# A fused attention and feed-forward kernel: its planner's order replaced by a table of placements

## The chip, the cores and the metric

The kernel runs on 1 core of one Trainium2 chip. The metric is the device time of one execution in microseconds (us), taken as the median of 3 runs. The kernel before has a median of 208.76 us (208.06 to 209.29).

The core has these engines, each with its own queue of instructions that runs in order: TensorE for matmuls (PE in the profile, PEld for its weight loads), VectorE (DVE), ScalarE (ACT), GpSimd (POOL) and SyncE (SP, which only issues DMAs here). PSUM, where matmuls write, has 8 banks. An instruction starts when it is at the head of its engine's queue and the semaphores that it waits for have been raised.

## The reference

```python
B, H, S, D = 4, 8, 768, 64            # n_sink = 4, window = 128
scores = scale * q @ k.T               # per batch and head
keep = (pos_k < 4) | (0 <= pos_q - pos_k < 128)
a = softmax(where(keep, scores, -1e9)) # over keys
x = merge_heads(a @ v)                 # (4, 768, 512)
xn = (x - mean) / sqrt(var + 1e-6) * g_ln
out = x + relu(xn @ w_ch1) @ w_ch2     # 512x2048, then 2048x512; float32 out
```

Each query sees the 128 latest keys and the first four keys of its batch (the sinks). What follows is a layer norm without a bias, two layers of weights with a ReLU between them, and the sum with x.

## The kernel before

**Tiles and chunks.** The 3072 tokens are 24 tiles of 128 tokens (t = 0 to 23), six for each batch, and 12 chunks of two tiles (c = 0 to 11; chunk c has tiles 2c and 2c+1). All matmuls are in bf16 with sums in fp32. The three big inputs are loaded tile by tile in bf16 (by GpSimd's queue, which casts on the way; L589 for v, L626 and L687 for q and k), apart from the first tile, whose q and k come in fp32 on SyncE (L620) and are cast on chip (cast0, cast1, L637).

**Attention.** For each tile or chunk: q and k are transposed (on TensorE for chunks 0 to 3, L645 and L672, with copies out of PSUM named ev..., L595; by DMA on SyncE from chunk 4, helper L569); scores (sc, L754 for one tile, L802) go into a pair of PSUM banks; ScalarE makes the exponents (ex, L758 and L814); VectorE or GpSimd multiplies by a mask (mk, L761, L826, L821); the values are weighted by matmuls (av, L854); the sinks have scores, exponents and values of their own (sx and sv, L714 and L721). ev10 and ev11 are the copies of the transposed q and k of chunk 1, ev010 and ev011 those of the second tile. For the sinks, kts is a small buffer of the sinks' keys (kts0 is the copy at L695), pick is a constant that spreads them, and vc holds the sinks' values of the later batches: vc0 clears it (VectorE, L511) and vcd stands for 16 small loads into it on SyncE (L535).

**Layer norm.** VectorE divides by the sum (rc, L868, and x, L870) and takes mean and variance (bn, L874, and ag); GpSimd takes the power -0.5 (rs, L882; it reads the constant mhalf); xc (L885) is x less the mean. Then x is transposed: for chunks 0 and 1 on TensorE (trx, L893) with a copy that multiplies by g (evx, L907, by the four columns gt, L531); from chunk 2 by a DMA on SyncE (trx, L569). The result is xnt.

**The two layers.** Layer 1 makes ph0 to ph7 (L1020 by tile for chunks 0 and 1, so that ph0_0 needs tile 0 alone and ph0_1 tile 1; L1027 later; the name is ph, then the chunk, then the number). From chunk 4, half of them is replaced by seven smaller products m1 to m7 with fewer multiplications (L958), whose sums run on VectorE, ScalarE and GpSimd. A ReLU (rl, L1037 on ScalarE, L1039 on VectorE) moves each ph to hq. From chunk 2 layer 2 is seven products p1 to p7 (L1109, 8 matmuls each) in the place of eight: sums s1 to s4 of blocks of hq (VectorE, L1092) and differences of w2 are multiplied; tm (L1123) adds x, o (L1130) makes the last sum of a quarter of 128 tokens by 256 columns, each on VectorE. For p6 the sum s2 of both halves is needed, and s2 needs s1 and the ReLUs of ph4 to ph7. o11_0 to o11_3 are the four quarters of chunk 11.

**Stores.** All go out on SyncE: whole tiles of 128x512 in fp32 (256 KB; L1070, L1159) and quarters of 128x256 (128 KB; L1154) for the first tile of some chunks and both tiles of the last. st20 and st21 are the stores of tiles 20 and 21 (chunk 10), st220, st221, st232 and st233 the four quarters of tiles 22 and 23. At the very end, gsum and late are single tiny matmuls, and guard is a check of the softmax sums; if it failed, a slow general version in a branch would run. It doesn't for these inputs.

**What sets the order.** The body doesn't issue instructions as it goes. It describes 1137 operations with `P.op(name, engines with durations, priority, emit, reads, writes, ...)`, and `Plan.run` then places them: a list scheduler with a cost of each operation on each engine that may run it, a priority (mostly the time at which it is due), rings of buffers, latencies between engines, and a model of the DMA queues. It gives each operation an engine and a start, and a buffer slot for each buffer. At the end all operations are sorted by that start and emitted, and each engine runs its own in that order. So a planned start is no command to wait: it sets only who stands ahead of whom on an engine. Gaps of TensorE in the first 24 us of the plan are filled with junk matmuls (L1236) that no operation needs.

Of the kernel before, what the change touches and what calls it, by code (L numbers as in the profile page):

```python
# [64 lines left out]
class Plan:  # L65


    SEM = 0.035
    TO_PE = 0.11
    PE_DRAIN = 0.18  # L70
    SWITCH = 0.095
    LANES = 8
    SHARED = 36.0
    MIXED = 1e9
    DMA_BUSY = {}

# [31 lines left out]
    def lat(self, src, dst):  # L108
        if src.eng == "PE" and src.dma is None:
            return -self.PE_DRAIN if dst == "PE" else self.SEM  # L110
        return self.TO_PE if dst == "PE" else self.SEM

    WINDOW = {"PE": 0.2, "ACT": 0.25, "DVE": 0.25, "POOL": 0.25, "SP": 0.0}

    def run(self):
        free = {"PE": 0.9, "ACT": 0.75, "DVE": 0.9, "POOL": 1.5, "SP": 0.75}
        lanes = {"POOL": [0.0] * self.LANES, "HW": [0.0] * self.LANES}
        n_dma = {"POOL": 0, "HW": 0}
        dma_free = {"POOL": 0.0, "HW": 0.0, "all": 0.0}
        mode = "n"  # L120
        ready = [o for o in self.ops if o.n_wait == 0]
        order = []
        tensor = sorted((o for o in self.ops if "PE" in o.engs), key=lambda o: (o.prio, o.seq))
        while ready:
            while tensor and tensor[0].start is not None:
                tensor.pop(0)
            head = tensor[0] if tensor else None
            cand = {}
            first = min([o.prio for o in ready for b in o.bufs if b.ring == "pair" and b.slot is None], default=1e9)
            for o in ready:  # L130
                if "PE" in o.engs and o is not head and o.prio >= PAR["strict"]:
                    continue
                need = [b for b in o.bufs if b.ring and b.slot is None]
                ok, avail, took = True, 0.0, {}
                for b in need:
                    used = [u for s in took.values() for u in s.units]
                    ss = [s for s in self.rings[b.ring] if not s.held and not any(u in used for u in s.units)
                          and not (s.lent and o.prio > first)]
                    if not ss:
                        ok = False  # L140
                        break
                    since = max([min(s.free_at for s in ss)] + [min(free[e] for e in o.engs) - 0.3])
                    s = min((s for s in ss if s.free_at <= since), key=lambda s: (s.rank, s.free_at))
                    took[b] = s
                    avail = max(avail, s.free_at)
                if not ok:
                    continue
                best = None
                for e, (occ, lat) in o.engs.items():
                    r = max([free[e], o.nb, avail + (self.TO_PE if e == "PE" else self.SEM)]  # L150
                            + [d.end + self.lat(d, e) for d in o.deps])
                    if e == "PE" and o.mode_in != mode:
                        r = max(r, free[e] + self.SWITCH)
                    if o.dma is not None:
                        q = "POOL" if e == "POOL" else "HW"
                        r = max(r, lanes[q][n_dma[q] % self.LANES])
                    if best is None or r + lat < best[0] - 1e-9:
                        best = (r + lat, e, r)
                cand.setdefault(best[1], []).append((best[2], o, took))
            if not cand:  # L160
                stuck = sorted(ready, key=lambda o: o.prio)[:8]
                raise RuntimeError("plan stuck: " + ", ".join(
                    f"{o.name}[{','.join(b.name for b in o.bufs if b.ring and b.slot is None)}]" for o in stuck))
            e = min(cand, key=lambda e: min(c[0] for c in cand[e]))
            t0 = min(c[0] for c in cand[e])
            st, o, took = min((c for c in cand[e] if c[0] <= t0 + self.WINDOW[e]), key=lambda c: (c[1].prio, c[1].seq))
            for b, s in took.items():
                b.slot = s
                s.take()
            o.eng, o.start = e, st  # L170
            occ, lat = o.engs[e]
            free[e] = st + occ
            if e == "PE":
                mode = o.mode_out
            if o.dma is None:
                o.end = st + lat
            else:
                busy, first, last = o.dma
                q = "POOL" if e == "POOL" else "HW"
                if st < self.MIXED:  # L180
                    at = max(st + occ + first, dma_free[q], dma_free["all"] if st < self.SHARED else 0.0) + busy
                    dma_free[q] = dma_free["all"] = at
                    o.end = at + last
                else:
                    real = self.DMA_BUSY.get(o.dma, busy)
                    other = dma_free["HW" if q == "POOL" else "POOL"] > st + occ + first
                    at = max(st + occ + first, dma_free["all"]) + real
                    dma_free[q] = dma_free["all"] = at
                    o.end = at + last + max(0.0, busy - real) + (PAR["mix"][q == "POOL"] if other else 0.0)
                lanes[q][n_dma[q] % self.LANES] = o.end  # L190
                n_dma[q] += 1
            for b in o.bufs:
                b.left -= 1
                if b.left == 0 and b.ring:
                    b.slot.give(min(u.start for u in b.users), max(u.end for u in b.users))
            ready.remove(o)
            order.append(o)
            for s in o.succ:
                s.n_wait -= 1
                if s.n_wait == 0:  # L200
                    ready.append(s)
        assert len(order) == len(self.ops), "cycle in the plan"
        order.sort(key=lambda o: (o.start, o.seq))
        return order


def pe(us):
    return {"PE": (us, us + Plan.PE_DRAIN)}

# [15 lines left out]
SW = (0.9, 0.7, 0.9)  # L225
# [7 lines left out]

Plan.DMA_BUSY = {SW: 1.03, HW_X: 0.55}

LOW, HIGH = 1e-9, 1e9
NEG = -1e30
NEVER = -1e9

# [134 lines left out]
def kernel(  # L374
# [157 lines left out]
    for g in range(4):  # L532
        for hh in range(4):
            p0 = 32 * g + NS * hh
            P.op(f"vcd{g}{hh}", {"SP": (0.3, 0.3)}, 3.2 + 0.01 * (4 * g + hh), lambda e, p0=p0, h=4 * (g % 2) + hh: nc.sync.dma_start(  # L535
                vc[p0:p0 + NS, 1:B, 0:64], v[1:B, h, 0:NS, :].rearrange("b s d -> s b d")),
                reads=[Bc["vc"]], writes=[Bc["vcd"]], dma=HW_T, nb=30.0)
# [67 lines left out]
    def chunk(c):  # L605
# [74 lines left out]
        else:  # L680
            for x, (nm, src) in enumerate((("k", k), ("q", q))):
                for i in range(2):
                    nat = Buf(f"{nm}n{c}{i}", "nat")
                    ap = src[b, :, 256 * R + 128 * i:256 * R + 128 * (i + 1), :].rearrange("h p d -> p h d")
                    soon = c >= PAR["half"] + 3 and x == 0 and i < PAR["soon"]
                    loads[2 * c + i, nm] = P.op(f"{nm}ld{c}{i}", {"POOL": (0.87, 0.9)}, ld + 0.01 * i + 0.1 * x,
                         lambda e, nat=nat, ap=ap: G.dma_start(nat.t, ap), writes=[nat], dma=SW if c < 6 else (*SW[:2], PAR["llag"]), after=behind(c, 0 if soon else 1))  # L687
                    loads[2 * c + i, nm].soon = soon
                    P.op(f"tr{nm}{c}{i}", {"SP": (1.2, 1.2)}, d + 0.01 * i, lambda e, nat=nat, i=i, x=x: dma_t(
                        T.t[:, :, x, 128 * i:128 * i + 128], nat.t.rearrange("p h d -> p (h d)")),  # L690
                        reads=[nat], writes=[T], dma=HW_X, after=[scores[c - 1]])
# [152 lines left out]
    def value(c, i, pes, ps, d, part, srcs, po=None):  # L844
# [49 lines left out]
        if c >= PAR["x_by_dma"]:  # L894
            P.op(f"trx{t}", {"SP": (1.2, 1.2)}, d + 0.5, lambda e: dma_t(xnt_b[c].t[:, :, 128 * i:128 * i + 128], xc.t),
# [110 lines left out]
    def mlp(c):  # L1006
# [38 lines left out]
        for i in range(2):  # L1045
# [5 lines left out]
            for f in range(parts):  # L1051
# [17 lines left out]
                P.op(f"st{t}{f}", {"ACT" if parts == 2 and not f else "SP": (0.35, 0.4)}, T + 4 * i + 3.6,  # L1069
# [4 lines left out]
    def wino(c, T, hq, h1, quick):  # L1074
# [76 lines left out]
        for half in (0, 2, 3, 1) if c == NC - 1 else (0, 1) if c in PAR["split"] else ():  # L1151
            t, sl = 2 * c + half // 2, slice(256 * (half % 2), 256 * (half % 2) + 256)
            b, r = t // RB, t % RB
            P.op(f"st{t}{half}", {"SP": (0.35, 0.4)}, 3000.0 + half % 2 if c == NC - 1 else u(6), lambda e, i=half // 2, b=b, r=r, sl=sl: nc.sync.dma_start(  # L1154
                out[b, 128 * r:128 * (r + 1), sl], ots[i].t[:, sl]), reads=[oo[half]], hold=[ots[half // 2]], dma=HW_S)
        for i in () if c == NC - 1 else (1,) if c in PAR["split"] else (1, 0):
            t = 2 * c + i
            b, r = t // RB, t % RB
            P.op(f"st{t}", {"SP": (0.35, 0.4)}, u(5 if i else 6), lambda e, i=i, b=b, r=r: nc.sync.dma_start(  # L1159
# [120 lines left out]
```

## Time and profile before

| | |
|---|---|
| median of 3 runs | 208.76 us (208.06 to 209.29) |
| span of the profiled execution | 206.6 us |
| so around the span | 2.16 us |
| TensorE busy | 199.4 us, 97% of the span |
| VectorE busy | 179.6 us, 87% |
| ScalarE busy | 119.7 us, 58% |
| GpSimd busy | 118.7 us, 57% |
| DMA over the span | 27.55 MB, 133 GB/s in the mean |

The profile is of one execution. Its own time isn't given apart from its span; the median of the runs, taken without a profile, stands 2.16 us above that span. A line of code in the profile is that of the kernel before, given as L and its number. A row of a timeline is start, duration, engine, line, operation, and output<-inputs by the buffers' names; a bracket at its end is the time for which the engine had stood idle and what ended that. A row of the groups has the busy time and the mean in ns behind the bar, and then the idle time before the group. The buffer names join many operations: `one` and `pair` are the PSUM rings, `kq` the transposed q and k, `xnt` the transposed tokens, `hq` the hidden layer, `hs` the sums s1 to s4, `ot` the output.

### The profile page before, as it was taken

How to read it: one execution, taken by the hardware profiler on the slowest of the kernel's cores; microseconds unless marked ns; L12 is line 12 of the kernel's file. 1: busy time of each engine (PE TensorE's matmuls, PEld its weight loads, DVE VectorE, ACT ScalarE, POOL GpSimd, SP SyncE). 2: the span in 40 equal slices, each digit the busy share in tenths (PEclk: the TensorE clock that was granted, in tenths of full speed). 3: DMA queues.
4: the chain of work that ended last, by engine and by line, in shares of the span. 5: the costliest groups of instructions: out<-in, count | busy, mean ns of one | idle time of the engine just before them, and what ended most of it. 6: DMA issues, size and time to landing. Idle time of an engine off the chain costs nothing.

```text
span 206.6 us, 6790 instructions
## 1 busy us (share of the span) xinstructions
PE 199.4 (97%) x2766; PEld 165.6 (80%) x2766; DVE 179.6 (87%) x437; ACT 119.7 (58%) x187; POOL 118.7 (57%) x170
## 2 busy tenths in 40 slices
PE   6888999999999999999999999999999999999994
PEld 2557996674698897898998988988988988988993
DVE  7589769899599899899989989989989989998693
ACT  3649477839555655666486486485486585560620
POOL 7977475279039029959649949968627229125000
PEclk9999999999999999999999999999999999999999
DMA  5999999999999999999999999899976411210302
GB/s 117 146 195 195 197 181 205 199 158 171 186 200 124 124 191 101 121 174 101 175 152 137 113 159 143 109 171 114 194 117 101 128 33 23 106 32 19 108 27 84
DMA packets 101341, 27.55 MB, mean 133 GB/s; under 512 B 89652, under 2 KB 99128, under 8 KB 101304
## 3 DMA queue, kind: packets, MB, share of 16 engines
q0 software_dynamic: 67712, 13.37, 81.7%
q1 hardware_dynamic: 33304, 13.43, 34.1%
q8 instruction: 22, 0.36, 0.7%
q10 hardware_dynamic: 288, 0.26, 0.4%
q14 instruction: 15, 0.12, 0.2%
HBM read 27.31 MB, written 6.29 MB: 163 GB/s over the span
## 4 chain that ended last, share of the span: by engine, by line
PE 90%; DMA 3%; DVE 3%; POOL 2%; issue 0%; DVEq 0%
PE one L1109 31%; PE one L1027 20%; PE one L958 12%; PE one L1058 7%; PE one L1020 7%; PE pair L854 5%; PE pair L802 4%; DMA n4b<-in_q_dram 3%; PE one L672 1%; PE pair L721 1%; POOL nat L626 1%; PE one L714 1%; DVE xnt L907 1%; DVE kq L595 1%; POOL vn L589 0%; DVE st L874 0%
## 5 line engine op out<-in xcount | busy, mean ns | idle before, releaser
L1027 PE MATMUL one<-xnt,w 128*128 128x256 bf16 x384 | 46.8, 273 | 0.0
L814 ACT ACTIVATE pe<-pair 128x1024 bf16<-128x1024 f32 (+1 forms) x40 | 36.3, 963 | 18.2 <-PE pair L802 18.2
L1037 ACT ACTIVATE hq<-one 128x512 bf16<-128x512 f32 x58 | 33.4, 590 | 17.9 <-PE one L1020 9.4
L1027 PEld LDWEIGHTS <-w 128*128 128x128 bf16 x384 | 36.3, 98 | 4.0
L1109 PEld LDWEIGHTS <-hs 128*128 128x128 bf16 x320 | 31.0, 98 | 4.0
L882 POOL TENSOR_SCALAR st<-st 128x1 f32<-128x1 f32 x24 | 6.4, 266 | 44.4 <-DVE rec L868 27.5
L826 DVE TENSOR_TENSOR pe<-pe,mask 128x1024 bf16<-128x1024 bf16 (+1 forms) x35 | 27.1, 799 | 1.6 <-ACT pe L814 1.4
L969 ACT COPY tz<-one 128x512 f32<-128x512 f32 x24 | 13.9, 585 | 20.6 <-PE one L958 19.2
L1109 PEld LDWEIGHTS <-hq 128*128 128x128 bf16 x240 | 22.2, 98 | 4.1 <-issue 0.5
L589 POOL DMA_DIRECT2D vn<-in_v_dram x24 | 21.9, 922 | 2.2 <-DMA w<-in_moe_w_ch_dram 1.2
L983 ACT ACTIVATE hq<-hq 128x512 bf16<-128x512 bf16 x24 | 15.1, 630 | 13.1 <-DVE hq L980 12.6
L1109 PE MATMUL one<-w,hq 128*128 128x256 bf16 x160 | 19.2, 273 | 0.0
L980 DVE TENSOR_TENSOR hq<-one,tz 128x512 bf16<-128x512 f32 x24 | 16.4, 684 | 1.9 <-PE one L958 1.0
L1130 DVE TENSOR_TENSOR ot<-one,tm 128x256 f32<-128x256 f32 x40 | 15.9, 412 | 2.1 <-PE one L1109 1.8
L1123 DVE TENSOR_TENSOR tm<-one,x 128x256 f32<-128x256 f32 x40 | 16.6, 414 | 1.2 <-PE one L1109 1.1
L870 DVE TENSOR_TENSOR x<-pair,rec 128x512 bf16<-128x512 f32 x24 | 16.6, 691 | 0.8
L874 DVE BATCH_NORM_STATS2 st<-x 128x6 f32<-128x512 bf16 x24 | 16.5, 687 | 0.2
L1020 PE MATMUL one<-xnt,w 128*128 128x128 bf16 x256 | 16.0, 219 | 0.5 <-DVE xnt L907 0.5
L687 POOL DMA_DIRECT2D nat<-in_q_dram x16 | 14.2, 893 | 3.7 <-DMA w<-in_moe_w_ch_dram 3.7
L938 POOL TENSOR_TENSOR xt<-xnt 128x256 bf16<-128x256 bf16 x16 | 12.2, 778 | 7.1 <-DMA xnt<-xc 7.0
L687 POOL DMA_DIRECT2D nat<-in_k_dram x16 | 14.8, 928 | 2.4 <-DMA w<-in_moe_w_ch_dram 2.4
L1020 PEld LDWEIGHTS <-w 128*128 128x128 bf16 x256 | 14.6, 98 | 1.6 <-issue 0.8
(130 smaller groups left out, 387.7 us busy)
## 6 DMA issues: line engine op xcount, KB each, us to landing
out_dram<-ot SPq DMA_DIRECT2D x17, 256.0 KB
w<-in_moe_w_ch_dram POOLq DMA_DIRECT2D x8, 512.0 KB, 12.8
vn<-in_v_dram POOLq DMA_DIRECT2D x24, 128.0 KB, 6.9
nat<-in_k_dram POOLq DMA_DIRECT2D x17, 128.0 KB, 4.6
nat<-in_q_dram POOLq DMA_DIRECT2D x17, 128.0 KB, 4.9
out_dram<-ot SPq DMA_DIRECT2D x14, 128.0 KB
kq<-nat SPq DMA_TRANSPOSE x32
xnt<-xc SPq DMA_TRANSPOSE x20
```

What stands on the lines that cost most here:

```text
L589: loads[b * RB + r, "v"] = P.op(f"vld{t}", {"POOL": (0.87, 0.9)}, prio, lambda e: G.dma_start(bv.t[:, :, 0:64], v[b, :, 128 * r:128 * (r + ...
L687: lambda e, nat=nat, ap=ap: G.dma_start(nat.t, ap), writes=[nat], dma=SW if c < 6 else (*SW[:2], PAR["llag"]), after=behind(c, 0 if soon e ...
L814: P.op(f"ex{c}{hp}", {"ACT": act(2 * n)}, d + 0.1 + 0.05 * j, lambda e, pp=pp, pb=pb: nc.scalar.activation(pb.t[:, :, 0:n], pp.t[:, :, 0:n ...
L826: V.tensor_mul(pb.t[:, :, 0:n], pb.t[:, :, 0:n], mm),
L870: P.op(f"x{t}", {"DVE": dve(512)}, d + xo + 0.11, lambda e: V.tensor_tensor(x.t.rearrange("p (a h c) -> p a h c", a=2, c=64), pv()[:, :, : ...
L874: P.op(f"bn{t}", {"DVE": fix(0.60)}, d + xo + 0.12, lambda e: V.bn_stats(st.t[:, 8:14], x.t), reads=[x], writes=[st, mv])
L958: nc.tensor.matmul(b.t[:, 128 * h:128 * h + 128], lhsT=lt[:, kk, 128 * h:128 * h + 128], rhs=rh[:, kk, :], start=first and h == 0 and kk = ...
L1020: nc.tensor.matmul(ph.t[:, 128 * s:128 * s + 128], lhsT=w1[u // 2][:, j, 128 * s:128 * s + 128], rhs=xnt.t[:, j, 128 * (u % 2):128 * (u % ...
L1027: nc.tensor.matmul(ph.t[:, 256 * s:256 * s + 256], lhsT=w1[ht // 4][:, j, 128 * (ht % 4):128 * (ht % 4 + 1)], rhs=xnt.t[:, j, :], start=j ...
L1037: nc.scalar.activation(hg.t[:, u % 4, :], ph.t, AF.Relu)
L1109: nc.tensor.matmul(at(r), lhsT=get(left, g)[:, v, s, :], rhs=rhs, start=first and n == 0, stop=n == 7, skip_group_check=True)
L1123: return P.op(f"tm{name}_{c}", {"DVE": dve(256, 1.14)}, pr - PAR["kp"], lambda e: V.tensor_tensor(tm[name].t, at(r), xs[i].t[:, sl], op=AL ...
```

## The change

`Plan.run` no longer schedules. It reads a table, SCHEDULE, with one entry for each of the 1137 operations in the order in which the body describes them: a letter for the engine (P TensorE, A ScalarE, V VectorE, G GpSimd, S SyncE) and a start in hundredths of a us. A second table, SLOTS, gives the buffer slot of each of 639 buffers; these are the slots that the planner chose as well. The operations are the same, and so are what they read and write; what changes is the order on each engine, and the engine of 24 operations. The planner's constants go, and the durations of SyncE's operations in the descriptions become a little longer (they matter only for where the junk matmuls may stand).

```diff
     def run(self):
-        free = {"PE": 0.9, "ACT": 0.75, "DVE": 0.9, "POOL": 1.5, "SP": 0.75}
...
-        order.sort(key=lambda o: (o.start, o.seq))
-        return order
+        engines = dict(P="PE", A="ACT", V="DVE", G="POOL", S="SP")
+        table = SCHEDULE.split()
+        assert len(table) == len(self.ops)
+        for o, entry in zip(self.ops, table):
+            o.eng, o.start = engines[entry[0]], int(entry[1:]) / 100
+            o.end = o.start + o.engs[o.eng][1]
+        for b, n in zip(dict.fromkeys(b for o in self.ops for b in o.bufs if b.ring), "".join(SLOTS.split())):
+            b.slot = self.rings[b.ring][int(n, 36)]
+            for u in b.slot.units:
+                u.lives.append((min(o.start for o in b.users), max(o.end for o in b.users)))
+        return sorted(self.ops, key=lambda o: (o.start, o.seq))
...
+SCHEDULE = """
+V90 V103 V116 V144 G150 G180 V192 A4220 V162 V150 V156 V330 V212 V218 V224 V1183 V231 V240 V4715 V3680 V416 V1083
+V1653 V4427 V336 S181 P915 V1193 S3719 S3755 S3791 S3827 S3863 S3899 S3935 S3971 S4007 S4043 S4079 S4115 S4151 S4187
...
+P18807 V18916 S20459 S20369 G18652 G18893 G18737 G18821 P18762 A18828 P19071 A19137 P18895 V18961 A19187 P18939 A19038
...
+V19520 V19439 V19596 V19485 V19673 V19871 V19760 P19528 V19637 P20076 V20185 P19615 V19724 P19726 V19835 P19814 V19923
+P19901 V20134 V20010 P19989 V20098 S20234 S20324 S20279 S20414 V18110 P18400 V18551 P20164
...
-            P.op(f"vcd{g}{hh}", {"SP": (0.3, 0.3)}, 3.2 + 0.01 * (4 * g + hh), lambda e, p0=p0, h=4 * (g % 2) + hh: nc.sync.dma_start(
+            P.op(f"vcd{g}{hh}", {"SP": (0.36, 0.36)}, 3.2 + 0.01 * (4 * g + hh), lambda e, p0=p0, h=4 * (g % 2) + hh: nc.sync.dma_start(
```

What moves, by the order of the two plans:

- **VectorE, start.** Before, the copies cast1, ev0001 and then the chain rc0, x0, bn0, ag0, xc0, ev10, evx0. After: cast0, ev0000, ev0011, ev010, rc0, x0, ev011, pick, bn0, kts00, gt, ag0, xc0, kts0, evx0, rc1, x1, bn1, a mask, ag1, xc1, mhalf, evx1. ev10 is ScalarE's now.
- **ScalarE, start.** The dummy exponent tab, first before, has 42.20. The order is cast1, ev0010, ev0001, ex0_0, two of tile 1, ev10, ev11, ex2_0 and on.
- **GpSimd.** The first 40 operations keep their order; later loads of v, q and k have later entries.
- **SyncE.** The early loads are as before; the 16 vcd loads have 37.19 to 42.59, behind vc0 at 36.80 on VectorE; trx4 and trx5, the DMA transposes of chunk 2's tokens, have 42.95 and 45.91. The last entries are st16, st19, then st220 (202.34), st233, st232, st20, st221, st21 (204.59). Before, the last six are st21, st20, st220, st232, st233, st221, and st21 and st20 stand right behind their sums.
- **TensorE.** The first layer of chunk 2 stands behind av6 and av7, the values of chunk 3's tiles. The products of chunk 11 stand in the order p1, p7, p6, p4, p5, p3, p2; before, p1, p2, p7, p6, p4, p5, p3. gsum stands earlier.
- **VectorE, end.** The last sums are o11_2, o11_1, o11_3, o11_0.
- **Engines.** To ScalarE: cast1, ev0001, ev10, evx2, evx3, three of the w1g (columns of w1 times g, L1190), rl1_4, rl1_5, rl11_4. To VectorE: cast0, ev0000, rl0_5, rl0_7, rl1_0, rl1_3, rl2_4, rl3_4 and five of the w1g.

More of the change, by code (lines that the diff above doesn't have):

```diff
@@ L207, in pe @@
+PE_DRAIN = 0.18
 def pe(us):
-    return {"PE": (us, us + Plan.PE_DRAIN)}
+    return {"PE": (us, us + PE_DRAIN)}
 def act(n):
```

177 lines of the change are left out of this document (72 added, 105 removed).

## The prediction, made before the changed kernel was run

> **What bounds the kernel now.** I read the waits of TensorE first. From 19 us to 203.4 us that view has no row: TensorE never waits for another engine. A table of three stretches says the same (columns: stretch, length, then busy time and instructions of PE, PEld, DVE, ACT and POOL, granted clock, DMA share, GB/s).
>
> ```profile
> 0.00:18.75 18.75, 14.57 (x194) 9.14 (x195) 13.83 (x50) 10.21 (x14) 14.95 (x25) 1.00 1.29 160
> 18.75:203.41 184.66, 184.63 (x2570) 156.40 (x2569) 165.30 (x387) 109.46 (x174) 103.72 (x145) 1.00 1.18 131
> 203.41:206.60 3.19, 0.19 (x2) 0.09 (x2) 0.42 (x1) 0.00 (x0) 0.00 (x0) 0.97 0.29 94
> ```
>
> The middle is 184.63 us of matmul in 184.66 us, at full clock. The table moves operations and removes none. A new order can shorten only the head of 18.75 us and the tail of 3.19 us, and it can lengthen all three. Then the chain that ended last:
>
> ```profile
> 5.50 7.09 DMA n4b<-in_q_dram
> ...
> 13.41 1.23 DVE kq L595
> 14.63 0.60 DVE xnt L907
> ...
> 18.01 0.70 DVE xnt L907
> ...
> 18.75 1.05 PE one L1020 x16
> ...
> 184.07 6.38 PE one L1109 x56
> ...
> 197.29 6.13 PE one L1109 x56
> 203.45 0.44 DVE ot L1130
> ```
>
> Up to 12.60 us the head waits for a load, then mostly for VectorE; from 18.75 us all is TensorE; the last product is followed by one sum on VectorE and one store.
>
> The page gives a span of 206.6 us; the runs have a median of 208.76, so some 2.16 us lie around the span. I sum against 206.6 and add 2.16. The three runs differ by 0.6% (208.06 to 209.29); 0.5%, or 1.04 us, is about what a measurement of this kernel can tell from no change.
>
> **The tail (the likeliest loss).** Today the stores of tiles 20 and 21 leave at 190 to 191 us, two quarters of the last two tiles before 203, one at 203.35, and only the last quarter behind the last sum. In the table, SyncE's last six entries are st220 (202.34), st233, st232, st20, st221 and st21 (204.59), in that order, and st220 needs o11_0, which the table makes VectorE's last operation. So nothing of the last chunk, and neither tile of the chunk before, is stored until the last sum ends: 4 x 128 KB + 2 x 256 KB = 1 MB. Rows of SyncE's timeline, and two stretches in which stores run (last columns: DMA share, GB/s):
>
> ```profile
> 1.02 0.86 SPq L620 DMA_DIRECT2D n4a<-in_k_dram  x2
> 118.34 0.53 SPq L1159 DMA_DIRECT2D out_dram<-ot  x1
> 118.97 0.44 SPq L1154 DMA_DIRECT2D out_dram<-ot  x1
> 203.90 0.33 SPq L1154 DMA_DIRECT2D out_dram<-ot  x1
> 201.00:201.50 0.50, 0.50 (x8) 0.44 (x5) 0.50 (x2) 0.00 (x0) 0.00 (x0) 1.00 0.67 234
> 191.25:192.00 0.75, 0.75 (x16) 0.74 (x14) 0.00 (x0) 0.75 (x2) 0.00 (x0) 1.00 0.94 352
> ```
>
> A quarter (128 KB) fills 0.67 of 0.50 us, so 0.34 us of all engines; a whole tile at 352 GB/s takes 262 KB / 352 = 0.74. All six: 4 x 0.34 + 2 x 0.74 = 2.84 us, where today 0.34 follows the last issue. By the transfers alone the end moves by 2.5 us. By the issues: one store takes 0.33; six in a row aren't in the trace. Nearest rows: two loads in 0.86, so the second 0.44 behind the first; two stores 0.63 apart. Five more at 0.33, 0.44 or 0.63 are 1.65, 2.2 or 3.15, and the last one moves a whole tile, 0.40 longer: 2.05, 2.6 or 3.55. The larger of both limits holds: 2.5 to 3.55. I take **+2.6**, by the plain pair. The cover that hides the stores of 20 and 21 today is 12 us of matmuls; that cover is gone.
>
> **The head.** The table sends the copy of 1.23 us (ev10, on the chain) to ScalarE, behind which ev11 runs already; and it puts ev011, pick, kts00, gt and kts0 between x0 and evx0 on VectorE.
>
> ```profile
> 7.63 0.41 DVE L695 COPY kts<-kq 64x16 bf16<-64x16 bf16 x2
> 8.25 0.76 DVE L595 COPY kq<-one 128x512 bf16<-128x512 bf16 x2 [0.21 <-PE one L645]
> 9.32 0.16 DVE L531 COPY gt<-one 128x4 f32<-128x4 f32 x1 [0.31 <-PE one L529]
> 13.85 1.01 ACT L595 COPY kq<-one 128x1024 bf16<-128x1024 bf16 x1 [0.66 <-PE one L672]
> 15.23 1.02 ACT L758 ACTIVATE pe<-pair 128x1024 bf16<-128x1024 f32 x1 [0.36 <-PE pair L754]
> 16.68 1.07 PE L1020 MATMUL one<-xnt,w 128*128 128x128 bf16 x16
> 17.58 0.39 PE L893 MATMUL one<-ident,xc 128*128 128x128 bf16 x4
> ```
>
> VectorE loses 1.23 and gains 0.38 + 0.44 (pick: 0.17 + 0.27) + 0.14 + 0.16 + 0.41 = 1.5, all in front of evx0. ScalarE copies twice in a row: 13.40, then 14.3 to 15.3, so the first exponent (ex2_0) starts at 15.3 instead of 15.23. Layer 1 needs sc3_0 ahead of it on TensorE, which needs that exponent's PSUM pair, so ph0_0 stays at 16.7, trx1 behind it at 17.6, evx1 at 18.0 and ph0_1 at 18.75. Moved past each other, the parts give nothing: **0**, from -0.4 to +0.4. On POOL, rs0 now waits for mhalf, which comes late on VectorE (after xc1, some 17.5), and the loads queued behind it with it:
>
> ```profile
> 16.13 0.96 POOL L589 DMA_DIRECT2D vn<-in_v_dram  x1 [0.75 <-DMA w<-in_moe_w_ch_dram]
> 40.05 0.97 PE pair L854 x32
> ```
>
> That load of v starts 2.5 us later; it is used at 40 us, so this is hidden. The four casts and copies of the first tile that change engine wait for the same loads as now: 0.
>
> The dummy exponent that brings ScalarE's table (tab) moves from the start to 42.2, so the first copy (cast1) brings it.
>
> ```profile
> 1.95 1.28 ACT L481 ACT_TABLE_LOAD   x1 [1.95 <-PEq L1261]
> 5.04 0.62 ACT L637 CAST hq<-n4a 128x512 bf16<-128x512 f32 x1 [1.59 <-DMA n4a<-in_q_dram]
> 7.92 1.02 ACT L758 ACTIVATE pe<-pair 128x1024 bf16<-128x1024 f32 x1 [0.84 <-PE pair L754]
> 10.19 0.42 PE L854 MATMUL pair<-vn,pe 128*128 128x65 bf16 x8 [0.91 <-ACT pe L758]
> ```
>
> If the load stands ahead of cast1's waits it runs in ScalarE's idle time, as now. If behind them, the first exponent moves by at most 1.28; it ends at 8.94 today and its reader starts at 10.19 (the named releaser had long been done, so it waits for v), so 1.25 of it is covered: 0 either way. The Trainium skill, "ScalarE: Activation LUTs", section "What ACT_TABLE_LOAD costs", puts a switch of tables at some 1.28 us and a drain of 1.38 besides; by that the head would lose up to 1.4 and the time be 212.8. Here the next activation follows the load within 0.02 us, at 3.25, so the trace shows no such drain.
>
> **The middle.** The transposes of tokens on TensorE and SyncE, the six ReLUs and the scaled weights that change engine feed operations that lie microseconds later; TensorE's work is the same, with as many changes of tile position. Two places don't cancel by themselves. In chunk 10 seven products take 6.38 where seven without waits take 6.13: 0.25 of wait, which goes, since the table has the reader's sums (s3, s2) earlier and gsum ahead. In chunk 11, p2 moves from second to last, so from ph11_7 to p6 there are two products (2 x 0.876) where there were three.
>
> ```profile
> L1037 ACT ACTIVATE hq<-one 128x512 bf16<-128x512 f32 x58 | 33.4, 590 | 17.9 <-PE one L1020 9.4 <-PE one L1027 8.5
> L1092 DVE TENSOR_TENSOR hs<-hq 128x512 bf16<-128x512 bf16 x40 | 15.0, 418 | 0.8 <-ACT hq L1037 0.6
> ```
>
> Between them: the drain of ph11_7 (0.17, the overlap of the chain's rows), a ReLU of 0.59, s1, tm and s2 of 0.42 each and gaps of some 0.05, 2.0 in all against 1.75: 0.25 of wait comes. Net **0**, to +1 for such places that I didn't find: VectorE is busy for 165.30 of 184.66 us, so it has little to catch up with.
>
> The sinks' loads (16 on SyncE) move from 3.64 to behind vc0, some 38 us, and the transposes by DMA for chunk 2 queue behind them.
>
> ```profile
> 3.64 7.97 SPq L535 DMA_DIRECT2D vc<-in_v_dram  x16
> 44.45 2.29 SPq L569 DMA_TRANSPOSE xnt<-xc  x1
> 46.84 1.20 SPq L569 DMA_TRANSPOSE xnt<-xc  x1
> 54.34 1.91 PE L1027 MATMUL one<-xnt,w 128*128 128x256 bf16 x16
> 3.64:11.61 7.97, 6.95 (x66) 3.90 (x64) 5.04 (x19) 3.31 (x5) 7.52 (x11) 1.00 1.56 146
> 37.00:47.00 10.00, 10.00 (x131) 6.31 (x128) 9.20 (x21) 5.56 (x10) 5.93 (x9) 1.00 2.09 178
> vc<-in_v_dram SPq DMA_DIRECT2D x16, 3.0 KB
> ```
>
> They take 16 x 0.34 = 5.4 to 7.97 us of SyncE, so both transposes are issued by 47 to 50 instead of 48.04, for matmuls that start at 54.34 now and some 0.7 later in the table (two small av ahead of them). That holds while the loads land as fast as at the start: 0. Out of the head, their 48 KB at 146 GB/s free 0.33 us for the early loads; that is inside the head's -0.4.
>
> **Sum.** 206.6 + 2.6 + 0 + 0 = 209.2 of span, 211.4 with what lies around it.
>
> **Rivals.** *Not slower* (0.13): the 1.23 us that leave VectorE's part of the chain aren't filled again, because the five small operations fit into its waits (it idles 1.24 ahead of rc0) and the two copies on ScalarE overlap TensorE's score matmuls. Then ph0_1 starts 1.23 earlier, 0.33 more by the freed loads, and chunk 10's 0.25 goes: 211.4 - 1.8 = 209.6, no change by my bound. It decides from the point where evx1 ends before 17.7. Against it: ev011 stands behind x0 in the order, so rc0's wait can't be used, and ex2_0 is held to 15.3.
>
> *Slower still, at SyncE* (0.12): the sinks' loads meet a busier DMA (share 2.09 against 1.56), so that the second eight wait for the first; at twice the 7.97 us, 38 + 16 + 3.5 = 57.5 plus landing, and layer 1 of chunk 2 waits 2 to 3 us instead of none: 213.9. This is also the case in which the token transposes don't stand well ahead of layer 1, as the change says they do.
>
> *Table of ScalarE exposed* (0.04): 1.28 - 1.25, so 211.4 by the rows.
>
> *More waits in the middle* (0.13): VectorE's new order misses its partner in several chunks, +1 to +3: 213.4. A further 0.03: head and tail both better than any bound above.
>
> **Numbers.** The forecast has 0.55: 211.4, by itself from 210.9 (all -0.4 of the head) to 212.9 (issues 0.63 apart, +0.4). The range 209.9 to 213.9 takes in the slower rivals and part of the first. Faster by over 0.5% (under 207.72): 0.03. Within 0.5%: 0.13. Slower (over 209.8): 0.84.
>
> **What would show it.** Tail: six stores behind the last sum, a third row of 5.7 us instead of 3.19. Middle: 184.7 us of matmul without a row of waits but at p6 of chunk 11. Head: ph0_1 at 18.3 to 19.2. Wrong would be a tail as long as now, ph0_1 before 17.7, or TensorE waiting for the transposes of chunk 2.

## The result, and the profile after

The changed kernel takes 214.38 us in the median (214.08 to 214.82, 4 runs), the kernel before 208.66 (208.06 to 209.29, 4 runs): a ratio of 1.0276, 95% interval 1.0248 to 1.0304. It is slower by 5.72 us. The forecast was slower by 2.6, and the range ended at 213.9, half a us short. Ratios are of a kernel's fast executions alone, which leaves out slower ones (four of the ten of the run with the table for the first half, below).

The profiled execution has a span of 212.7 us, 6.1 more than before. The table of three stretches of the kernel after, cut where TensorE's last product ends (columns as in the prediction):

```profile
0.00:18.75 18.75, 15.51 (x198) 9.20 (x198) 11.74 (x47) 10.94 (x14) 13.35 (x23) 1.00 1.29 161
18.75:205.43 186.68, 185.63 (x2573) 155.97 (x2572) 166.91 (x392) 107.93 (x178) 104.62 (x148) 1.00 1.18 126
205.43:212.70 7.27, 0.10 (x2) 0.00 (x0) 0.42 (x1) 0.00 (x0) 0.00 (x0) 0.79 0.43 149
```

The head is as long as it was. The middle is 186.68 instead of 184.66, so 2.02 longer, and TensorE is no longer busy all through it. The tail is 7.27 instead of 3.19, so 4.08 longer. Together that is the 6.1.

**Tail.** SyncE's timeline of after; a row that joins three stores stands first, the third of them by itself second:

```profile
205.91 2.55 SPq L1135 DMA_DIRECT2D out_dram<-ot  x3
...
206.76 1.69 SPq L1135 DMA_DIRECT2D out_dram<-ot  x1
208.50 0.43 SPq L1140 DMA_DIRECT2D out_dram<-ot  x1
208.98 0.45 SPq L1135 DMA_DIRECT2D out_dram<-ot  x1
209.47 0.46 SPq L1140 DMA_DIRECT2D out_dram<-ot  x1
```

All six stores stand behind the last sum, which ends at 205.88. Their issues take until 209.93, that is 4.02 us where one store took 0.33 before. Five more at some 0.43 with gaps of 0.05 are 2.4. The rest is that one of them took 1.69. From the last issue to the end it is then 2.73 us, before 2.37, since the last store now is a whole tile. The view of the DMA queues over 205 to 212.6 us shows what else ran there (queue, kind: packets, MB, share of 16 engines):

```profile
q1 hardware_dynamic: 864, 1.05, 39.5%
q8 instruction: 1, 0.02, 1.1%
q14 instruction: 2, 0.02, 0.7%
```

q1 carries the stores; q8 and q14 fetch instructions. The q8 packet (16 KB) begins at 206.81 and takes 1.34, just when the long issue runs. It follows TensorE's branch, not SyncE's own. Two rows of the view of the branch's line (TensorE's queue, then SyncE's; the last times are the start):

```profile
L1221 PEldq COMPARE_BRANCH  x1: 398/398/398, 205.7 to 205.7; - x1
L1221 SPq COMPARE_BRANCH  x1: 53/53/53, 210.0 to 210.0; - x1
```

SyncE branches only when all its stores are issued. In every trace of a kernel with the branch, a 16 KB packet of q8 begins 1.1 to 1.6 us after TensorE's branch.

**Middle.** Two stretches, first of before, then of after:

```profile
100.00:140.00 40.00, 40.00 (x607) 35.62 (x605) 36.65 (x87) 26.41 (x44) 30.86 (x43) 1.00 1.25 144
140.00:180.00 40.00, 40.00 (x595) 35.42 (x593) 37.71 (x87) 24.24 (x40) 19.48 (x29) 1.00 0.73 104
```

```profile
100.00:140.00 40.00, 39.19 (x584) 34.15 (x582) 37.55 (x82) 25.25 (x42) 29.42 (x42) 1.00 1.33 131
140.00:180.00 40.00, 39.77 (x581) 34.17 (x582) 37.16 (x88) 23.96 (x39) 22.16 (x32) 1.00 0.93 103
```

TensorE's busy time falls to 39.19 and 39.77 of 40, and it gets 23 and 14 instructions fewer done. That idle time is only 1.04; the ends of matmuls are modelled, so a part of a wait can count as busy. The waits are therefore measured from the start of one operation to the start of the next. Seven steps of after are longer than the median of their kind: by 0.31 (a value matmul of chunk 7), 0.26 and 0.56 (p4 and p5 of chunk 6), 0.33 (ph7_6), 0.29 (chunk 10's values), 0.17 (p5 of chunk 9) and 0.26 (chunk 11's values), 2.2 in all. The 0.25 of chunk 10 that before lost is gone. What remains is 1.9 of the 2.0. The largest wait, by the timelines of TensorE, VectorE and GpSimd in the kernel after:

```profile
129.80 0.71 PE L1090 MATMUL one<-n4b,hs 128*128 128x256 bf16 x5 [0.40 <-DVE tm L1104]
...
128.56 0.85 DVE L1073 TENSOR_TENSOR hs<-hq,hs 128x512 bf16<-128x512 bf16 x1
129.33 0.41 DVE L1104 TENSOR_TENSOR tm<-one,x 128x256 f32<-128x256 f32 x1
...
128.43 1.50 POOL L919 TENSOR_TENSOR xt<-xnt 128x256 bf16<-128x256 bf16 x2
```

p5 waits for a tm, which reads a PSUM bank of the ring that p5 writes. That tm stands behind an s4 sum, and the sum takes 0.85 while GpSimd makes two of its token sums xt. The same place before:

```profile
127.79 0.41 DVE L1123 TENSOR_TENSOR tm<-one,x 128x256 f32<-128x256 f32 x1
128.12 0.74 DVE L1092 TENSOR_TENSOR hs<-hq,hs 128x512 bf16<-128x512 bf16 x2
...
128.85 1.80 POOL L938 TENSOR_TENSOR xt<-xnt 128x256 bf16<-128x256 bf16 x2 [0.30 <-DMA xnt<-xc]
```

There the tm comes first, both s4 together take 0.74, and xt begins when they are done. By groups (before, then after), the s4 sums have a mean of 486 ns before and 589 after, the large masks 908 before and 818 after:

```profile
L1092 DVE TENSOR_TENSOR hs<-hq,hs 128x512 bf16<-128x512 bf16 x20 | 9.3, 486 | 0.0
L826 DVE TENSOR_TENSOR pe<-pe,mask 128x1024 bf16<-128x1024 bf16 x23 | 20.4, 908 | 0.7 <-ACT pe L814 0.7
```

```profile
L1073 DVE TENSOR_TENSOR hs<-hq,hs 128x512 bf16<-128x512 bf16 x20 | 11.6, 589 | 0.0
L807 DVE TENSOR_TENSOR pe<-pe,mask 128x1024 bf16<-128x1024 bf16 x23 | 18.5, 818 | 0.3 <-ACT pe L795 0.3
```

So long durations on VectorE aren't new. In before they fall more on the masks, and there TensorE doesn't wait.

**Head and chunk 2.** Rows of the timelines of ScalarE, TensorE and SyncE of after:

```profile
5.01 1.28 ACT L618 ACT_TABLE_LOAD   x1 [5.01 <-DMA n4a<-in_q_dram]
6.31 0.62 ACT L618 CAST hq<-n4a 128x512 bf16<-128x512 f32 x1
...
16.64 1.07 PE L1001 MATMUL one<-xnt,w 128*128 128x128 bf16 x16
...
18.75 0.62 PE L1001 MATMUL one<-xnt,w 128*128 128x128 bf16 x8
...
47.42 2.61 SPq L550 DMA_TRANSPOSE xnt<-xc  x2
...
54.76 2.02 PE L1008 MATMUL one<-xnt,w 128*128 128x256 bf16 x17
```

The load of ScalarE's table does stand behind the wait of the first cast, and TensorE waits 0.7 us for that cast. By ph0_0 at 16.64 it is made up, and ph0_1 starts at 18.75, to the hundredth as before. The transposes of chunk 2 are issued by 50.0, and its layer 1 starts at 54.8 without a wait.

### The profile page after: what moved, and what is told of

Read it like the earlier page. It is cut to its first block, busy times and chain, and to the rows that moved or that the text cites. A ratio compares the mean times of both kernels' runs of the same rounds, so it can differ in the third digit from the quotient of the medians.

```text
span 212.7 us, 6759 instructions
## 1 busy us (share of the span) xinstructions
PE 201.2 (95%) x2769; PEld 165.2 (78%) x2769; DVE 179.1 (84%) x439; ACT 118.9 (56%) x191; POOL 118.0 (55%) x170
## 5 line engine op out<-in xcount | busy, mean ns | idle before, releaser
L1008 PE MATMUL one<-xnt,w 128*128 128x256 bf16 x384 | 46.0, 272 | 0.2 <-DVE ot L1111 0.2
L1018 ACT ACTIVATE hq<-one 128x512 bf16<-128x512 f32 x55 | 31.7, 597 | 20.1 <-PE one L1008 12.2
L1008 PEld LDWEIGHTS <-w 128*128 128x128 bf16 x384 | 36.7, 98 | 4.3 <-issue 0.3
L1090 PEld LDWEIGHTS <-hs 128*128 128x128 bf16 x320 | 29.9, 98 | 5.7 <-issue 0.9
L807 DVE TENSOR_TENSOR pe<-pe,mask 128x1024 bf16<-128x1024 bf16 (+1 forms) x35 | 26.3, 764 | 0.3 <-ACT pe L795 0.3
L1090 PEld LDWEIGHTS <-hq 128*128 128x128 bf16 x240 | 22.7, 98 | 3.7 <-issue 0.3
L570 POOL DMA_DIRECT2D vn<-in_v_dram x24 | 22.4, 935 | 0.5 <-issue 0.5
L1073 DVE TENSOR_TENSOR hs<-hq 128x512 bf16<-128x512 bf16 x40 | 15.8, 420 | 2.9 <-ACT hq L1018 1.5
L864 POOL TENSOR_TENSOR st<-st,mhalf 128x1 f32<-128x1 f32 x24 | 14.3, 596 | 5.0 <-DVE mhalf L503 3.1
```

The costliest lines, as they stand in the source:

```text
L570: loads[b * RB + r, "v"] = P.op(f"vld{t}", {"POOL": (0.87, 0.9)}, prio, lambda e: G.dma_start(bv.t[:, :, 0:64], v[b, :, 128 * r:128 * (r + ...
L807: V.tensor_mul(pb.t[:, :, 0:n], pb.t[:, :, 0:n], mm),
L1008: nc.tensor.matmul(ph.t[:, 256 * s:256 * s + 256], lhsT=w1[ht // 4][:, j, 128 * (ht % 4):128 * (ht % 4 + 1)], rhs=xnt.t[:, j, :], start=j ...
L1018: nc.scalar.activation(hg.t[:, u % 4, :], ph.t, AF.Relu)
L1073: P.op(f"{n}_{c}{g}", {"DVE": dve(512, 0.52)}, T - PAR["sp"][g] + PAR["sq"][i], lambda e, n=n, x0=x0, x1=x1, g=g, op=op: V.tensor_tensor(s ...
L1090: nc.tensor.matmul(at(r), lhsT=get(left, g)[:, v, s, :], rhs=rhs, start=first and n == 0, stop=n == 7, skip_group_check=True)
```

## The experiments

Theory T (tail): the stores behind the last sum, one of them held up by a fetch of instructions at the branch that ends the program, are 4.1 us. Theory C (middle): VectorE's bf16 operations are held up while GpSimd's token sums run, and the table brings them together at places where TensorE then waits, 2.0 us. Rivals: the tail's extra 1.3 belongs to the program's end whatever the stores do; VectorE's order alone makes the middle's waits; the first half's order costs as well. A time of before that stands beside a run is that of its own batch.

**The six stores early again.** The same loop serves the next run, in the kernel before.

```diff
     order = P.run()
+    move = {"st21": 188.6, "st20": 189.6, "st232": 199.7, "st221": 201.2, "st233": 201.7, "st220": 202.3}
+    for o in order:
+        if o.start > 150:
+            o.start = move.get(o.name, o.start)
+    order.sort(key=lambda o: (o.start, o.seq))
```

> The changed kernel with its last six stores put back behind their own sums; all else as in the table. The trace of after has 4.02 us of store issues behind the last sum (0.34 + 0.43 + 1.69 + 0.43 + 0.45 + 0.46 and gaps) and 2.77 from the last issue to the end, where before has 0.33 and 2.37. Theory (the stores, with the one issue of 1.69 that ran into a fetch of instructions at the end of the program, are 4.1 of the 5.7 lost): 214.4 - 4.1 = 210.3, a stretch of 3.2 us behind TensorE's last product. Rival (the 1.3 us that the long issue has too much belong to the end of the program and stay whatever the stores do): 211.6, with 4.5 us behind the last product.

Measured: 212.75 us against 208.66, ratio 1.0179 (1.0127 to 1.0230). The stretch behind the last product is 5.16, neither of the two values:

```profile
205.54:210.70 5.16, 0.11 (x2) 0.01 (x2) 0.42 (x1) 0.00 (x0) 0.00 (x0) 0.79 0.26 83
```

Since p2 is last and o11_0 behind it, three quarters still stand together at the end; the issues are short, but the data come late. Of the run's stores and fetches from 205.5 to 210.6 us, in the trace's packets, all but nine packets of the last quarter are out by 207.5. Then come the fetches (q8 at 207.34 for 1.2 us, q14 at 207.57 and 207.86). These nine go out from 208.53 to 209.2, and the q8 packet ends at 208.54. So the fetch seems to hit a store in its transfer too, though no run of this order leaves the branch out, and my two-sided expectation had missed the order of the products.

**Before, with the six stores late.**

```diff
+    move = {"st221": 300.0, "st233": 300.1, "st232": 300.2, "st20": 300.3, "st220": 300.4, "st21": 300.5}
```

> The kernel before with its last six stores put behind its last sum, in the order of the table but for the quarter that waits longest, which goes first; all else as before. Theory of the collision (when TensorE has ended, the program branches, instructions are fetched, and a store issue that meets the fetch takes 1.7 instead of 0.43): one of the six issues is long again, and the time is 208.7 + 4.1 = 212.8. Rival (only the plain price: five more issues at 0.43 with gaps of 0.05, and 0.4 for the whole tile that lands last): 208.7 + 2.8 = 211.5, no issue over 0.6. My forecast had 2.6: 211.3.

Measured: 213.94 us against 208.66, ratio 1.0219 (1.0170 to 1.0268). SyncE's timeline of this run:

```profile
205.42 1.31 SPq L1154 DMA_DIRECT2D out_dram<-ot  x3
206.77 0.99 SPq L1159 DMA_DIRECT2D out_dram<-ot  x1
207.80 1.44 SPq L1154 DMA_DIRECT2D out_dram<-ot  x1
209.29 0.44 SPq L1159 DMA_DIRECT2D out_dram<-ot  x1
```

Two issues are long, 0.99 and 1.44, not the third but the fourth and fifth: q14 fetches at 206.80, q8 at 207.27. The stretch behind the last product (204.93 in this execution) is 7.76, that is 4.57 more than before's. Six late stores by themselves, without the rest of the table, cost the whole of the tail's loss. The plain price alone (2.8) is out. The time is 1.1 over the 212.8 that the theory of the collision gave: two issues are held up and not one, and some 0.7 us of the loss lies ahead of the tail and isn't explained.

**The table without the branch.**

```diff
-    tc.mark_branch_hint_location("all_is_well", engines=[mybir.EngineType.PE, mybir.EngineType.DVE])
...
-    bad = nc.values_load(flag, min_val=0, max_val=128 * NT * H)
-    with tc.If(bad > 0, label="all_is_well"):
...
-        general(tc, nc, slots, pairs, ones, ident_f, ident, w1, w2, mhalf, g_s, g_r, q, k, v, out, scale)
```

> The changed kernel without the slow general version and the branch to it at the end; that version is left out, and for these inputs it doesn't run. Theory of the collision: without the branch TensorE fetches no instructions at 206.8, the third store's issue takes 0.43 instead of 1.69, and the time falls by 1.3 and by what the branch itself takes (0.5 between the last store and the closing semaphores): 212.6 to 213.1. Rival (the long issue comes from the stores themselves, the third in a row): the issue stays at 1.7 and the time at 213.9 to 214.4.

Measured: 212.96 us against 208.66, ratio 1.0191 (1.0140 to 1.0242). SyncE's timeline, the table from TensorE's last product on, and the only queue that moved anything from 205 to 211 us:

```profile
205.60 1.30 SPq L1135 DMA_DIRECT2D out_dram<-ot  x3
206.95 0.45 SPq L1140 DMA_DIRECT2D out_dram<-ot  x1
207.44 0.45 SPq L1135 DMA_DIRECT2D out_dram<-ot  x1
207.93 0.45 SPq L1140 DMA_DIRECT2D out_dram<-ot  x1
```

```profile
205.10:211.10 6.00, 0.13 (x3) 0.03 (x2) 0.42 (x1) 0.00 (x0) 0.00 (x0) 0.81 0.49 175
```

```profile
q1 hardware_dynamic: 864, 1.05, 48.6%
```

No fetch, and no issue over 0.45, so three stores in a row don't make a long issue by themselves. The tail is 6.00, so 1.27 less than in after, and 2.8 more than before. That splits the tail: 2.8 for six late stores as such, 1.27 that goes with the branch and its fetch. Nearly all of the 1.27 is the time of the issues, 2.78 here and 4.02 in after.

**The end of chunk 11 as before** (29 entries of the table, name, then old and new entry):

```diff
-p2_11 P20076   o11_0 V20185   st220 S20234   st221 S20414   st20 S20369   st21 S20459
+p2_11 P19643   o11_0 V19814   st220 S19863   st221 S20254   st20 S18974   st21 S18906
...
```

> The table, but the end of chunk 11 (its products, sums and stores, from p1 on) and the stores of chunk 10 in the order of before: 28 entries. The first run with early stores still had three quarters behind one another at the end, since p2 stands last, and the last rows of the last quarter landed only behind a fetch of instructions (1.2 us). Theory (the tail's loss is the stores that come late, by their place and by the place of p2, and nothing of the program's end): the stretch behind TensorE's last product falls from 7.25 to 3.2 us, and the time from 214.4 to 210.3. Rival (the fetch at the end costs whatever the order): 4.5 us or more behind the last product, 211.6 or more.

Measured: 210.37 us against 208.60, ratio 1.0087 (1.0064 to 1.0110). From TensorE's last product on:

```profile
205.84:209.00 3.16, 0.19 (x3) 0.09 (x2) 0.42 (x1) 0.00 (x0) 0.00 (x0) 0.84 0.29 94
```

3.16, as before's 3.19, and the time is the 210.3 of theory T. The tail is settled. What is left over before, 1.8 us, is the middle.

**Table for the first half, order of before for the second** (534 entries behind chunk 5's p1):

```diff
-m5_6 P11492   mk72 V11259   s4_61 V12608   tmt6_6 V12662   p5_6 P12728
+m5_6 P11515   mk72 V11274   s4_61 V12694   tmt6_6 V12624   p5_6 P12741
...
```

> The table up to chunk 5's first product of layer 2 (some 107 us), the order and engines of before for the 534 operations behind it, tail included. Theory (the 2.0 us that TensorE ends later come from single waits for VectorE in chunks 6 to 9, and nothing from what lies ahead of them): 208.7, within 0.4, and TensorE's last product ends at 203.4 within 0.4. Rival (the first half's order leaves VectorE behind, and it is paid for later): 209.7 to 210.7, with waits of TensorE in chunks 6 to 9 in this kernel too.

Measured: ratio 1.0049 (1.0006 to 1.0092) to before's 208.66, that is 209.7 us. By the number the rival's. The view of TensorE's waits has none for a tm any more, and a new one at the seam:

```profile
PE pair L772 <- DMA kq<-nat: 0.9, 1, 0.9
```

The scores of chunk 8 wait for a transposed q or k, whose transposes were queued by two plans that don't fit together. This run doesn't decide on the first half. The runs with the short sums do.

**GpSimd's sums cut short** (4 of 128 columns are computed, the rest of each sum is left out, and its buffers are cleared once by GpSimd; the kernel before got the same edit):

```diff
-            G.tensor_tensor(st.t[:, 16:17], st.t[:, 17:18], mhalf, op=ALU.pow)),
+            G.tensor_tensor(st.t[:, 16:17], st.t[:, 17:18], mhalf, op=ALU.pow),
+            *[G.memset(z.tile, 0.0) for z in P.rings["xt"] if t == 8]),
...
-                right(n), right(x0), right(x1), op=ALU.subtract), reads=[xnt] + [got[x] for x in (x0, x1) if x[0] == "t"],
+                right(n)[:, :, 0:4], right(x0)[:, :, 0:4], right(x1)[:, :, 0:4], op=ALU.subtract), reads=[xnt] + [got[x] for x in (x0, x1) if x[0] == "t"],
```

> The changed kernel with the 32 sums of GpSimd on the tokens (xt, some 0.8 to 1.1 us each) cut to 4 of 128 columns; the rest of these sums is left out and the two buffers are cleared once. In the trace of after TensorE waits for VectorE six times between 115 and 178 us, 2.0 us in all, and ahead of each stands a bf16 operation of VectorE that took about twice as long (0.85 for 0.42, 1.15 for 0.67) while such a sum ran on GpSimd. Theory (VectorE and GpSimd hold each other up, and the table puts more of VectorE's short bf16 sums under GpSimd's): the waits go for the most part, 214.4 - 1.5 to 2.0 = 212.4 to 212.9. Rival (VectorE's order itself makes them): at least four of the six waits and 213.7 or more stay.

> The kernel before with the same 32 sums cut to 4 columns, the rest left out. By both theories nothing: TensorE doesn't wait there in before; 208.7 within 0.5. If it falls by over 0.5, the sums cost before something too, and the run beside it is to be read by the difference.

Measured: the table so cut 214.74 us against 208.60, ratio 1.0305 (1.0282 to 1.0328); before so cut 208.03, ratio 0.9972 (0.9943 to 1.0000). By the time, theory C seems to fail. TensorE's waits in the cut table say why it doesn't:

```profile
PE one L1091 <- DVE hs L1074: 2.5, 2, 2.2
```

None of the waits of 115 to 178 us is left. A wait of 2.2 us at 80 us and a second of 0.2 at 98 us are new, the first some 2.5 us behind the clearing, which took GpSimd from 75.74 to 77.57. I had put a cost of my own into the experiment, as the next run bears out.

**The same, cleared by VectorE**, alone and together with the end as before:

```diff
-    constant("vc0", "DVE", 0.27, -54, lambda e: (V.memset(vc, 0.0), V.memset(vc[:, :, 64:65], 1.0)), writes=[Bc["vc"]])
+    constant("vc0", "DVE", 0.27, -54, lambda e: (V.memset(vc, 0.0), V.memset(vc[:, :, 64:65], 1.0),
+                                                   *[V.memset(z.tile, 0.0) for z in P.rings["xt"]]), writes=[Bc["vc"]])
```

> The changed kernel with GpSimd's 32 sums xt cut to 4 of 128 columns, as in the first run with short sums, but the two buffers are cleared by VectorE in its idle time at 33 us and not by GpSimd at 75 us: in that first run the six waits of 115 to 178 us were gone, but TensorE waited 2.8 us at 79 to 97 us, where the clearing stood. Theory (contention of GpSimd's sums with VectorE's bf16 operations): no wait of TensorE over 0.2 from 75 to 180 us, and 214.4 - 2.0 to 2.7 = 211.7 to 212.4. Rival (the waits are those of the order, and had only moved to the clearing): some 2 us of waits again, at 213.9 to 214.7.

> The table with the end of chunk 11 and the stores of chunk 10 as in before, and GpSimd's sums cut short as in the run beside it (the rest of them is left out). If tail and contention are the whole loss and add up: 210.4 - 2.0 to 2.7 = 207.7 to 208.4, that is the time of before with short sums (208.0) within 0.5. If something of the first 110 us costs as well, 209 or more.

Measured: 212.78 us against 209.32 alone, ratio 1.0187 (1.0108 to 1.0267); with the end as before 208.52, ratio 0.9949 (0.9917 to 0.9980). The two stretches of the first of them:

```profile
100.00:140.00 40.00, 40.00 (x606) 35.51 (x605) 36.69 (x85) 25.47 (x43) 25.22 (x40) 1.00 1.36 134
140.00:180.00 40.00, 40.00 (x597) 35.01 (x592) 36.30 (x91) 23.84 (x40) 15.10 (x32) 1.00 0.79 102
```

TensorE is busy all through again, with as many instructions as in before. VectorE's same s4 and GpSimd's cut sums, in this run's timelines:

```profile
128.91 0.41 DVE L1074 TENSOR_TENSOR hs<-hq,hs 128x512 bf16<-128x512 bf16 x1
...
129.58 0.84 POOL L920 TENSOR_TENSOR xt<-xnt 128x8 bf16<-128x8 bf16 x2
```

0.41 instead of 0.85. The cut sums come later here and don't run beside it, so this row alone doesn't say that a cut sum is harmless. The masks of 128x1024 on VectorE do, counted in the traces: in after, six that ran beside a full sum took 1.01 us in the mean and ten with nothing of GpSimd beside them 0.68; in this run, four beside a cut sum took 0.68. VectorE's order is still the table's, and GpSimd's own masks, which also slow an s4 sum (to 0.86 at most in both traces), are still there.

The interval of this one run is wide (it reaches into that of the result), so its time alone wouldn't decide; a wait of 0.2 us at 96 us stayed from the first cut. The pair with the end as before does decide: 1.0087 (1.0064 to 1.0110) with the full sums, 0.9949 (0.9917 to 0.9980) with the short ones. That is 1.4% or 2.9 us, each against before in its own batch; the spans of the two profiled executions differ by 1.6, so the size is known only roughly. In before the same cut gives 0.3%. And with both causes gone the table stands where the cut kernel before stands (0.9949 and 0.9972, intervals overlapping), so the first half costs nothing that shows. One thing isn't told apart: with the short sums GpSimd's later operations, its masks among them, come earlier, which may help TensorE as well.

**VectorE in the order of before** (58 entries, chunks 5 to 9):

```diff
-s4_60 V12859   s4_61 V12608   tmt6_6 V12662   mk82 V12698   mk83 V12794
+s4_60 V12662   s4_61 V12698   tmt6_6 V12608   mk82 V12794   mk83 V12859
...
```

> The table with VectorE's operations of chunks 5 to 9 around layer 2 (sums s, tm, o, and for chunks 5 to 8 the masks of the attention beside them) in the order of before within the same places: 58 entries; GpSimd as in the table. Rival of the run with short sums (it is the order): the waits go, 212.4 to 212.9. Theory of the contention: only the wait of 0.56 at p5 of chunk 6 goes, where s4 stands ahead of tm, and new ones may come: 213.6 to 214.4.

Measured: 217.12 us against 208.60, ratio 1.0406 (1.0375 to 1.0437), worse than both expectations. TensorE's waits:

```profile
PE pair L824 <- DVE pe L796: 2.4, 4, 0.8
PE one L1079 <- DVE ot L1100: 0.7, 2, 0.5
```

The value matmuls now wait for masks, which this order has later, while TensorE's order is still the table's. VectorE's old order isn't good in itself; it belongs to TensorE's old order.

**GpSimd in the order of before**, the end as before too (43 of 62 places):

```diff
-xtt0_7 G12805   xtt2_7 G12733   vld20 G12497   kld100 G13355
+xtt0_7 G12666   xtt2_7 G12738   vld20 G12966   kld100 G12173
...
```

> The table with the end as in before, and GpSimd's operations of chunks 5 to 9 in the order of before (43 of its last 62 places change); VectorE as in the table; nothing left out. If GpSimd's order alone brings its sums under the wrong operations of VectorE: waits of TensorE below 0.8 us, 208.7 to 209.2. If it is the pairing of both engines' orders, which neither order alone restores: 209.8 to 211.5, with the slow operations of VectorE at other places.

Measured: 211.40 us against 209.32, ratio 1.0106 (1.0040 to 1.0171), not told apart from the 1.0087 without this edit. TensorE waits at other places:

```profile
PE one L1079 <- DVE tm L1093: 1.6, 2, 1.0
```

Neither engine's old order alone, among all the rest of the table, takes the waits away. That both orders together set them is in line with this, but no run here has just these two changed.

**The sums on VectorE**, the end as before too (32 entries, and the engine in the description):

```diff
-xtt0_7 G12805   xtt1_7 G12890
+xtt0_7 V12805   xtt1_7 V12890
...
```

> The table with the end as in before, and the 32 sums xt on VectorE instead of GpSimd at the same places; nothing left out. VectorE gains 32 x 0.3 = 9.6 us of work and loses the 5.6 us by which its operations are stretched under these sums in the trace of after. Theory of the contention with room to spare: 208.6 to 209.4. Rival (VectorE, at 92 to 96% from 100 to 180 us, has no room for 4 us more and waits at the head of its queue for the transposed tokens): 210.6 to 213.

Measured: 210.29 us against 209.32, ratio 1.0060 (1.0026 to 1.0094); against 1.0087 (1.0064 to 1.0110) the intervals overlap, so a gain isn't shown. Measured against before, it lies between the two expected times. By groups, a sum costs VectorE 282 ns where GpSimd needed 779, and the s4 sums are back at 498:

```profile
L908 DVE TENSOR_TENSOR xt<-xnt 128x256 bf16<-128x256 bf16 x16 | 4.5, 282 | 0.5 <-DMA xnt<-xc 0.4
...
L1062 DVE TENSOR_TENSOR hs<-hq,hs 128x512 bf16<-128x512 bf16 x20 | 9.8, 498 | 0.0
```

The hold-up by the sums is gone, but VectorE has the work instead. No run with the whole computation came out ahead of the kernel before.

## Why the prediction was wrong

The sign was right and so was the likeliest place; the size was 2.6 of 5.72, and two steps failed.

**Tail: +2.6, measured +4.1.** The mechanism was right: six stores, all behind the last sum. By the run without the branch their own price is 2.8, so the plain pair (0.44 an issue) was a good choice. The failing step is that the sum had no term for what else the DMA engines do there: "The larger of both limits holds: 2.5 to 3.55" counted issues and transfers and left out the fetch of instructions behind the branch, 1.27. In before the last store's last packet ends at 205.27, and the fetches begin at 205.28 and 205.85, so they meet no store. But the trace of before had marks that I passed by: the row of 44.45 in the prediction has a transpose of 2.29 us beside one of 1.20, and a q8 packet begins at 45.24. The same holds for the rest of that trace: nine transposes that a q8 packet overlaps by over 0.4 us took 1.5 to 2.4, the 40 without any overlap 1.2 to 1.3.

**Middle: net 0, measured +2.0.** The step read: "TensorE's work is the same", and operations that move "lie microseconds later". The 0.25 of chunk 10 went, as said; the 0.25 at p6 of chunk 11 didn't come. The failing step is that VectorE's operations were costed at their mean durations (0.42 for an s sum), as if a duration went with the operation wherever it stands. An s4 took 0.85 beside a sum of GpSimd and 0.41 without one. The rival "more waits in the middle" (0.13, +1 to +3) named the sign and the size; its reason, that VectorE "misses its partner", lacked GpSimd.

**Head: 0, right.** ph0_0 at 16.64 was forecast at 16.7, ph0_1 at 18.75 as forecast. **ScalarE's table** stood behind the first cast's wait and cost TensorE 0.7 us there, and nothing at ph0_0: the cover of 1.25 held. **The sinks' loads and chunk 2:** the transposes were issued by 50.0, the late end of the forecast (47 to 50), without a wait. **The range:** tail and middle both came out high, and their sum lay outside because the range took such losses one at a time. The forecast's own upper end of 212.9 is some 0.2 more than its terms give (211.4 + 0.95 + 0.4).

## What to carry to other kernels

Where a schedule is replaced, the tail is read first: what is queued behind the last operation, and what else the program does at that moment. A duration measured in one order is a property of the pair of engines: ask which operations of VectorE run beside GpSimd's, and compare pairs, not orders of one engine. An experiment that takes a suspected cost away must be checked in the trace for a cost that it brings.

## What the runs showed of the hardware

A branch at the end of the program brings a fetch of instructions, and stores that meet this fetch are held up: a store's issue took 1.69 instead of 0.43, or 0.99 and 1.44, and once a store's last packets went out some 1.8 us later than the others. Without the branch the fetch and the long issue went (issues of 0.45 at most). How the one holds up the other, no run here shows. The Trainium skill, "Runtime: NRT & Kernel Launch", section "Instruction fetch mechanics", says that a taken branch whose target isn't in the window forces a fetch before execution goes on. The trace agrees with the fetch (16 KB, 1.16 us after TensorE's branch in after), and adds that an engine that hasn't branched yet pays as well, here SyncE, whose own branch came at 210.0.

VectorE's bf16 sum of 0.42 us took 0.85 beside a sum of GpSimd on bf16 tokens, and 0.41 in the run with GpSimd's sums cut to 8 columns. Large masks took 1.01 beside a full sum and 0.68 beside a cut one. The fp32 operations with an operand in PSUM (tm, 0.41 in both kernels) didn't change. The Trainium skill, "SBUF — State Buffer", section "SBUF: two separate sides", says that VectorE and GpSimd share a pair of ports, which one of them holds for a whole instruction. The numbers are in line with that: the sum lost 0.43, less than one xt of 0.78. Which port it is, no run here shows.
